# Cosine attention and an MLP mixer: residuals from DMA transposes, ScalarE norms, a permuted weight and two score tiles

## The chip, the cores and the metric

The kernel runs on one core of one Trainium2 chip. Time is device microseconds (us) of one execution. A fast run and a slow run are told apart: a run counts as slow when it took over 1.5% longer than the fastest run of the same kernel. Verdicts use the fast runs alone, with a 95% interval. The medians and ranges given in the tables are of all runs, slow ones included.

The engines are PE (TensorE, the matmuls), PEld (its weight loads, which overlap the matmuls), DVE (VectorE), ACT (ScalarE), POOL (GpSimd) and SP (SyncE, which here only issues DMAs). PEclk is the TensorE clock that was granted, as a share of full speed.

## The reference, cut to what matters

```python
# q, k, v: (8 batches, 12 heads, 448 rows, 64), float32
q_n = q / (norm(q) + 1e-6);  k_n = k / (norm(k) + 1e-6)
attn = softmax(q_n @ k_n.T / 0.1)
x = (attn @ v)                        # heads side by side: (8, 448, 768)

h = relu(x.T @ w_tok1) @ w_tok2       # 448 -> 256 -> 448, along the rows
u = x + h.T                           # first residual
h2 = relu(u @ w_ch1) @ w_ch2          # 768 -> 1536 -> 768, along the columns
out = u + h2                          # second residual
```

## The kernel before: the parts that the change touches

The kernel works through 48 pairs of heads, six to a batch. The schedule has one *slot* per pair. A slot scores one pair, applies the softmax weights of the pair before it, does the token mix of an earlier pair, and feeds matmuls of the channel mix of an earlier batch in between. I call the time from the first score matmul of one pair to that of the next the length of a slot.

Everything is fp16 on PE, with fp32 in PSUM. Both residuals are added on PE, by multiplying with an identity matrix into the PSUM tile that already holds the other term:

```python
ps2 = tile_pool(name="ps2", bufs=1, space=PSUM)      # one score tile of four banks

def rnorms(n, p0=0, p1=HP):                          # 1 / (norm + eps)
    nc.scalar.activation(out=rn, in_=ssq, func=AF.Ln, bias=tiny[:])
    nc.scalar.activation(out=rn, in_=rn, func=AF.Exp, scale=0.5)
    nc.vector.tensor_scalar_add(out=rn, in0=rn, scalar1=EPS_NORM)
    nc.vector.reciprocal(out=rn, in_=rn)

def score(i, cg):                                    # twice per pair
    psS = ps2.tile([128, 2, 2, 512], FP32, tag="s")
    ...                                              # four matmuls of 448 columns
    nc.scalar.activation(out=pt[:, cg], in_=psS[0:SC, :, :, 0:S], func=AF.Exp, scale=inv_tau)

def m_tok2(i):                                       # u, transposed, for one pair
    for tt in range(TT):
        nc.tensor.matmul(psU[:], r[:, tt, :], w2t[:, tt, 0:S], start=(tt == 0), stop=False)
    for c in range(NCH):                             # x residual: four identity matmuls,
        nc.tensor.matmul(psU[:].rearrange("d (p c) -> d c p", c=NCH)[:, c, :],   # every 4th column
                         x[:, c, :], id16[:, ...], start=False, stop=(c == NCH - 1))
    nc.vector.tensor_copy(out=ut[:, dt, 0:S], in_=psU[:])      # (odd batches: two parts)

def m_ch2(b, m, dh):                                 # one output unit, 56 in all
    for ct in range(CT):
        nc.tensor.matmul(psF[:], rows(gt, ct), wc2t[:, ct, ...], start=(ct == 0), stop=False)
    for i in range(3):                               # u residual: three identity matmuls
        nc.tensor.matmul(psF[:, 128 * i:128 * (i + 1)], rows(ut, 3 * dh + i), id16[:],
                         start=False, stop=(i == 2))
    if dh == 0: nc.vector.tensor_copy(out=o[:, 0:DH], in_=psF[:])
    else:       nc.scalar.copy(out=o[:, DH:D], in_=psF[:])
```

From pair 12 on the normalized q and k are already transposed by the DMA (`dma_start_transpose` issued by SP). Before that PE transposes them.

## Time and profile before

| | before |
|---|---|
| time, median of 3 runs (range) | 456.56 us (456.43 to 456.67) |
| PE busy, matmuls | 408.4 us of 455.0, 4104 |
| first matmul of the hidden layer (psG) | 67.0 us |
| first output unit starts (psF) | 107.2 us |
| last matmul starts | 450.1 us |

The windows view cuts the execution into stretches. Columns are the stretch, its length, then for PE, PEld, DVE, ACT and POOL the busy us (and the number of instructions), the granted PE clock, the mean busy share of the 16 DMA engines (the times of their packets are summed, so in a short stretch it can read above 1), and GB/s. The cuts are the second slot, a point just before the first hidden layer, the first output unit, and the start of the last pair.

```profile
core 0: us, PE busy (x) PEld busy (x) DVE busy (x) ACT busy (x) POOL busy (x), PEclk, DMA share, GB/s
0.00:21.30 21.30, 3.73 (x26) 1.90 (x27) 10.47 (x17) 8.36 (x13) 9.01 (x18) 1.00 0.98 230
21.30:66.60 45.30, 32.76 (x422) 23.08 (x423) 28.34 (x69) 26.17 (x28) 33.30 (x34) 0.96 0.98 211
66.60:107.20 40.60, 30.55 (x297) 17.50 (x297) 26.08 (x45) 20.52 (x30) 29.35 (x29) 0.87 0.61 125
107.20:396.70 289.50, 287.75 (x2954) 175.05 (x2952) 128.81 (x305) 166.52 (x182) 141.83 (x137) 1.00 0.53 124
```

The reader should see two regimes. From 107.2 us on PE is idle for 289.50 - 287.75 = 1.75 us: it alone sets the time there, and any matmul removed should come off the total. In the 107 us before that, PE is busy for only 67, and the time is set by chains of other engines.

One such chain is seen in the timeline of before (start, length, engine, line, operation, output and input, and in brackets the idle time before it and what ended it):

```profile
53.48 1.22 DVE L155 TENSOR_REDUCE ssq_130<-sq_609 112x16 f32<-112x1024 f32 x1 [0.57 <-POOL sq_609 L150]
54.73 0.31 ACT L162 ACTIVATE rn_131<-ssq_130,tiny 112x16 f32<-112x16 f32 x1 [2.21 <-DVE ssq_130 L155]
55.19 1.65 ACT L210 ACTIVATE pt_719<-psS_0_720 112x1792 f16<-112x1792 f32 x1
56.89 0.93 PE L208 MATMUL psS_1_769<-qk_660 64*128 64x448 f16 x4 [2.30 <-ACT pt_719 L210]
...
71.36 6.27 DVE L164 TENSOR_SCALAR rn_382<-rn_382 112x16 f32<-112x16 f32 x1 [0.62 <-ACT rn_382 L163]
71.57 1.05 POOL L176 TENSOR_TENSOR qn_924<-qh_378,rn_382 112x512 f16<-112x512 f32 x1
...
76.57 1.03 POOL L150 TENSOR_TENSOR sq_931<-kh_702 112x512 f32<-112x512 f32 x1
77.55 0.88 POOL L112 DMA_DIRECT2D wc2t<-in_moe_w_ch_dram  x1
77.66 0.25 DVE L165 RECIPROCAL rn_382<-rn_382 112x16 f32<-112x16 f32 x1
78.56 0.53 PE L188 MATMUL pst_990<-id_83,kn_817 112*128 112x112 f16 x4 [8.11 <-DVE x_950 L225]
```

The first four lines are the circle that paces the opening. ACT waits for DVE's sum of squares before it can take the norm, only then does the exponential of 1792 columns, and the second group of scores waits for that exponential. The other lines are an accident in it. A tiny DVE instruction, the addition of epsilon on 16 columns, takes 6.27 us while POOL runs six computing instructions without a gap, and it ends as the last of them ends. PE waits 8.11 us, until DVE has done what stood behind it. This fits what the Trainium skill, "SBUF — State Buffer", section "🔬 SBUF: two separate sides", describes: DVE and GpSimd share one pair of ports under an exclusive lock, and the loser fully blocks.

### The profile page before, as it was taken

The numbers are of one execution on the slowest core, as the hardware profiler recorded it, in microseconds if no ns is written. First come the engines' busy times: TensorE is split into PE (matmuls) and PEld (weight loads), VectorE is DVE, ScalarE is ACT, GpSimd is POOL, SyncE is SP. The second block draws the span as 40 slices with busy tenths as digits, with TensorE's granted clock in tenths as the row PEclk, the third lists the DMA queues.
The fourth block names the chain that finished last, engine by engine and source line by source line (L and its number), as shares of the span: only waits on it lengthen the run. The fifth ranks groups of instructions, "written<-read, shape, count | busy, mean of one in ns | idle before, by whom it ended". The sixth has DMA issues, their size and how long they took to land.

```text
span 455.0 us, 9700 instructions
## 1 busy us (share of the span) xinstructions
PE 408.4 (90%) x4104; PEld 250.4 (55%) x4104; DVE 202.8 (45%) x458; ACT 236.8 (52%) x277; POOL 213.5 (47%) x216
## 2 busy tenths in 40 slices
PE   1377572899999999999999999999999999999995
PEld 0146451466655666556655666556656665566563
DVE  3656758565444354444534445446343433232000
ACT  3466543475466545675466455665565447630410
POOL 2686779391919265563838091926474330000000
PEclk9999987899999999999999999999999999999998
DMA  8999877752775169662685279733852233001012
GB/s 212 250 254 239 145 182 109 141 134 71 176 177 154 27 179 159 168 161 68 167 177 143 61 134 218 193 86 98 195 83 77 58 110 56 1 1 71 35 51 89
DMA packets 76411, 58.11 MB, mean 128 GB/s; under 512 B 36976, under 2 KB 72784, under 8 KB 76368
## 3 DMA queue, kind: packets, MB, share of 16 engines
q1 hardware_dynamic: 72704, 52.32, 48.0%
q0 software_dynamic: 3664, 5.18, 6.9%
q8 instruction: 32, 0.52, 0.5%
q14 instruction: 11, 0.09, 0.1%
HBM read 43.38 MB, written 11.01 MB: 120 GB/s over the span
## 4 chain that ended last, share of the span: by engine, by line
PE 80%; DVE 7%; ACT 6%; POOL 4%; issue 2%; DMA 1%; SPq 0%; ACTq 0%; POOLq 0%
DVE rn_382 L164 1%; DVE ssq_130 L155 1%; DVE ssq_381 L155 1%; DMA kh_104<-in_k_dram 1%; ACT pt_308 L210 1%; DVE ssq_118 L155 1%; DVE ssq_704 L155 0%; PE psG_2_1016 L269 0%; PE psF_1_0_3760 L288 0%; PE psF_1_0_2231 L288 0%; PE psF_0_0_2105 L288 0%; PE psF_2_1_1719 L288 0%; PE psF_1_0_5275 L288 0%; PE psF_1_1_1595 L288 0%; PE psF_0_1_1466 L288 0%
## 5 line engine op out<-in xcount | busy, mean ns | idle before, releaser
L269 PEld LDWEIGHTS <-wc1t 128*128 128x128 f16 x576 | 53.8, 101 | 45.1 <-issue 7.2
L233 PEld LDWEIGHTS <-w1t 128*128 128x128 f16 x384 | 22.7, 98 | 0.0
L288 PEld LDWEIGHTS <-gt_0_449 128*128 128x128 f16 x168 | 15.7, 98 | 10.9 <-issue 1.9
L288 PEld LDWEIGHTS <-gt_3_4834 128*128 128x128 f16 x168 | 15.9, 98 | 9.3
L288 PEld LDWEIGHTS <-gt_1_1784 128*128 128x128 f16 x168 | 15.8, 98 | 9.4 <-issue 0.4
L288 PEld LDWEIGHTS <-gt_2_3305 128*128 128x128 f16 x168 | 15.7, 98 | 9.5 <-issue 0.4
L188 PE MATMUL pst_156<-id_83,kn_154 112*128 112x112 f16 x4 | 0.6, 294 | 9.0 <-DVE kn_154 L176 9.0
L294 DVE COPY ost_0_6217<-psF_0_0_6218 128x384 f32<-128x384 f32 x1 | 0.6, 559 | 17.3 <-PE psF_0_0_6218 L291 17.3
L188 PE MATMUL pst_990<-id_83,kn_817 112*128 112x112 f16 x4 | 0.5, 286 | 8.1 <-DVE x_950 L225 8.1
L164 DVE TENSOR_SCALAR rn_382<-rn_382 112x16 f32<-112x16 f32 x3 | 6.6, 2206 | 1.9 <-ACT rn_382 L163 1.9
L176 POOL TENSOR_TENSOR qn_5263<-qh_4628,rn_4632 112x512 f16<-112x512 f32 x1 | 1.0, 1043 | 13.5 <-DVE rn_4632 L165 13.5
L176 POOL TENSOR_TENSOR qn_3745<-qh_3099,rn_3103 112x512 f16<-112x512 f32 x1 | 1.0, 1042 | 13.5 <-DVE rn_3103 L165 13.5
L176 POOL TENSOR_TENSOR qn_2216<-qh_1570,rn_1574 112x512 f16<-112x512 f32 x1 | 1.0, 1043 | 12.4 <-DVE rn_1574 L165 12.4
L176 POOL TENSOR_TENSOR qn_4510<-qh_3880,rn_3884 112x512 f16<-112x512 f32 x1 | 1.0, 1042 | 12.4 <-DVE rec_0_4542 L224 12.4
L176 POOL TENSOR_TENSOR qn_2981<-qh_2351,rn_2355 112x512 f16<-112x512 f32 x1 | 1.0, 1042 | 11.3 <-DVE rec_0_3013 L224 11.3
L176 POOL TENSOR_TENSOR qn_2611<-qh_1952,rn_1956 112x512 f16<-112x512 f32 x1 | 1.0, 1042 | 11.1 <-DVE rn_1956 L165 11.1
L176 POOL TENSOR_TENSOR qn_1839<-qh_1193,rn_1197 112x512 f16<-112x512 f32 x1 | 1.0, 1042 | 10.5 <-DVE rn_1197 L165 10.5
L176 POOL TENSOR_TENSOR qn_1452<-qh_808,rn_812 112x512 f16<-112x512 f32 x1 | 1.0, 1042 | 10.1 <-PE psO_0_1485 L221 10.1
L162 ACT ACTIVATE rn_107<-ssq_106,tiny 112x16 f32<-112x16 f32 x3 | 0.9, 307 | 9.1 <-DVE ssq_106 L155 9.1
L176 POOL TENSOR_TENSOR qn_4132<-qh_3481,rn_3485 112x512 f16<-112x512 f32 x1 | 1.0, 1044 | 9.6 <-DVE rn_3485 L165 9.6
L188 PEld LDWEIGHTS <-kn_154 112*128 112x128 f16 x4 | 0.3, 130 | 9.0 <-DVE kn_154 L176 9.0
L176 POOL TENSOR_TENSOR qn_4889<-qh_4246,rn_4250 112x512 f16<-112x512 f32 x1 | 1.0, 1042 | 9.0 <-DVE rn_4250 L165 9.0
(1681 smaller groups left out, 1266.8 us busy)
## 6 DMA issues: line engine op xcount, KB each, us to landing
wc1t<-in_moe_w_ch_dram POOLq DMA_DIRECT2D x2, 1152.0 KB, 10.9
wc2t<-in_moe_w_ch_dram POOLq DMA_DIRECT2D x2, 1152.0 KB, 9.5
qh_103<-in_q_dram SPq DMA_DIRECT2D x3, 224.0 KB, 4.3
kh_104<-in_k_dram SPq DMA_DIRECT2D x3, 224.0 KB, 4.6
vs_105<-in_v_dram SPq DMA_DIRECT2D x1, 672.0 KB, 7.0
qh_115<-in_q_dram SPq DMA_DIRECT2D x3, 224.0 KB, 8.1
kh_116<-in_k_dram SPq DMA_DIRECT2D x3, 224.0 KB, 8.3
vs_117<-in_v_dram SPq DMA_DIRECT2D x1, 672.0 KB, 10.7
```

Source lines behind the costliest of these rows:

```text
L155: nc.vector.tensor_reduce(out=half[i // HP]["ssq"][:, :, lo:lo + 2 * NCH], in_=pipe[i]["sq"][:], axis=AXX.X, op=ALU.add)
L162: nc.scalar.activation(out=rn, in_=ssq, func=AF.Ln, bias=tiny[:])
L164: nc.vector.tensor_scalar_add(out=rn, in0=rn, scalar1=EPS_NORM)
L176: eng.tensor_tensor(out=dst[:].rearrange("p c g e -> p g c e"), in0=src, in1=_bcast_free(rn, E), op=ALU.mult)
L188: nc.tensor.transpose(pst[:, a, c, :], src[:, c], id16[:SC, :SC])
L210: nc.scalar.activation(out=st["pt"][:, cg], in_=psS[0:SC, :, :, 0:S], func=AF.Exp, scale=inv_tau)
L233: nc.tensor.matmul(psR[:, tt, :], w1t[:, m, tt * 128:(tt + 1) * 128], st["x"][:, m, :], start=(m == 0), stop=(m == NCH - 1))
L269: nc.tensor.matmul(psG[:], wc1t[:, dt, ct * 128:(ct + 1) * 128], ut[:, dt, span(b)], start=(dt == 0), stop=(dt == DT - 1))
L288: nc.tensor.matmul(psF[:], rows(gt, ct), wc2t[:, ct, dh * DH:(dh + 1) * DH], start=(ct == 0), stop=False)
L294: nc.vector.tensor_copy(out=o[:, 0:DH], in_=psF[:])
```

## The change

The intent is to take work off PE where PE sets the time, and to unblock the opening.

1. Output residual. u is transposed back into rows by the DMA, 48 transposes issued by SP, and DVE adds it when it copies the output out of PSUM. The 168 identity matmuls go.
2. x residual. For pairs 12 to 41 the DMA transposes x into columns (30 transposes) and DVE adds it when it writes u. Four identity matmuls per pair go. For these pairs the second token matmul is one slot later.
3. w_tok2's columns are permuted once on POOL, so that the residual matmuls that stay write contiguous PSUM columns. DVE puts u's columns back in order, by writing with a stride of four elements.
4. Norms. Ln and Exp on ACT replace DVE's addition and reciprocal.
5. Scores. Two PSUM tiles of two banks in turn, in place of one of four, with exponentials of 896 columns in place of 1792.
6. Schedule. Norms, squares and loads of the opening come earlier.

```diff
+    X_DMA = range(12, NP_ALL - NPAIR)
-    ps2 = ctx.enter_context(tc.tile_pool(name="ps2", bufs=1, space=bass.MemoryType.PSUM))
+    ps2 = ctx.enter_context(tc.tile_pool(name="ps2", bufs=2, space=bass.MemoryType.PSUM))
...
+    def place_w2():
+        for tt in range(TT):
+            nc.gpsimd.tensor_copy(out=w2t[:, tt], in_=w2n[:, tt].rearrange("t (p c) -> t c p", c=NCH))
...
-        nc.vector.tensor_scalar_add(out=rn, in0=rn, scalar1=EPS_NORM)
-        nc.vector.reciprocal(out=rn, in_=rn)
+        nc.scalar.activation(out=rn, in_=rn, func=AF.Ln, bias=eps[:])
+        nc.scalar.activation(out=rn, in_=rn, func=AF.Exp, scale=-1.0)
...
+    def x_tpose(i):
+        st["xT"] = att.tile([128, NCH, 128], FP16, name=f"xT_{i}", tag="xT")
+        nc.sync.dma_start_transpose(out=st["xT"][:], in_=st["x"][:].rearrange("p c d -> p (c d)"))
...  # m_tok2
-            nc.tensor.matmul(psU[:].rearrange("d (p c) -> d c p", c=NCH)[:, c, :], st["x"][:, c, :],
+        for c in range(0 if by_dma else NCH):
+            nc.tensor.matmul(psU[:, c, :], st["x"][:, c, :], id16[:, LEAD[c]:LEAD[c] + SC],
+                             start=False, stop=(c == NCH - 1))
...
+                nc.vector.tensor_tensor(
+                    out=ut[:, dt, lo:lo + n].rearrange("d (p c) -> d c p", c=NCH)[:, c0:c1],
+                    in0=psU[:, c0:c1, p0:p1], in1=st["xT"][:, c0:c1, r + p0:r + p1], op=ALU.add)
...
+        nc.sync.dma_start_transpose(out=urt[b][:, dt, 0:n], in_=ut[:, dt, lo:lo + 128 * n])
...  # m_ch2
-        for i in range(3):
-            nc.tensor.matmul(psF[:, 128 * i:128 * (i + 1)], rows(ut, 3 * dh + i), id16[:],
-                             start=False, stop=(i == 2))
+        nc.vector.tensor_tensor(out=o[:, dh * DH:(dh + 1) * DH].rearrange("p (i d) -> p i d", i=3),
+                                in0=psF[:].rearrange("p (i d) -> p i d", i=3),
+                                in1=urt[b][:, 3 * dh:3 * dh + 3, j, :], op=ALU.add)
...  # schedule
-    sq_at = at({p: p - 3 if p < 10 else max(p - 6, 2 + p // 2) for p in range(3, NP_ALL)})
+    sq_at = at({p: p - 4 if p < 12 else max(p - 6, (p + 2) // 2) for p in range(4, NP_ALL)})
+    rn_at = at({p: p - 3 if p < 12 else (p + 4) // 2 for p in range(3, 15)})
+    EARLY = 8                        # slots in which the scores are issued in smaller parts
```

## The prediction

> **What bounds it now.** Windows view: from 109.3 us (first output unit) to 395.1 us TensorE (PE) is busy 284.0 of 285.8 us, DVE 127.5, ACT 164.9, POOL 141.8, DMA 0.54. Starts of successive matmuls follow at their column rate, so PE alone bounds this stretch and the tail. Before 109.3 it does not: PE idles 17.6 us up to 21.3, 12.5 up to 66.6, 8.1 up to 85.7. There each pair slot lasts about 6.5 us, on a circle in the timeline: DVE sum -> ACT Ln/Exp, DVE add and reciprocal -> ACT exponential of 1792 (1.66 us) -> second score group, which needs the single four-bank PSUM tile (PE waits about 2.2 us). At 71.4 us one DVE TENSOR_SCALAR on the norms takes 6270 ns instead of 175 while POOL runs without a gap; PE waits 8.1 us, and the recorded clock is half speed from 73.7 to 84.0. This agrees with the Trainium skill, "SBUF — State Buffer", "Terms": DVE and GpSimd share an exclusively locked port pair and the loser blocks.
>
> **PE work removed** (start-to-start times in the trace):
> - output residual: 168 matmuls x 55.8 ns = 9.4 us, all after 109 us;
> - x residual: about 342 ns per pair (strided columns, three of four at 95 ns) x 30 pairs = 10.3 us;
> - remaining 18 pairs: contiguous PSUM columns through permuted w2, 342 -> about 220 ns = 2.2 us.
> Together 22 us, nearly all in PE-bound time, so nearly all should appear.
>
> **Opening.** Norms leave DVE (no blocked TENSOR_SCALAR), are issued earlier, and score tiles alternate. I expect 5.5 us slots, the second slot at 17 us instead of 21.3, the first hidden-layer matmul near 57 instead of 67, and no stall at 70-79. That is worth 10 + 8 us plus some half-clock time, less what DMA gives back: it is already 0.98 busy to 66.6 us, and 10 MB of weights must still come. I count 14 us net.
>
> **Added.** 78 DMA transposes (48 u, 30 x). A present one takes 448 packets of 29 ns = 0.81 us of all 16 engines and 1.26 us of SP issue. DMA share in the steady stretch goes to about 0.8; SP issue per slot rises from about 4 us to 6.6 of a 7.4 us slot, in order, with waits. That is the danger: a late x transpose holds a PSUM bank and the in-order DVE. I charge 2-3 us. DVE gains the second output half (28 x about 0.56 us) and two to four adds for u, loses the norms (20 us): flat. ACT loses 13.4 us of output copies and gains fixed cost of 96 more exponentials, about 18 us: flat, off the path.
>
> **Sum.** 456.6 - 22 - 14 + 2.5 = 423 us. Range 409 to 438. Faster by over 2%: 0.96; same 0.03; slower 0.01.
>
> **What would show it.** PE start-to-start unchanged per kind and 288 matmuls fewer (4104 -> 3816); PE still over 97% busy from the first output unit to the end; steady slot 7.4 us instead of 7.94; no DVE instruction over 2 us; first hidden-layer matmul at 53 to 62 us; SP issuing 80-90% of the time, DMA 0.75-0.85; u copies waiting on x transposes in few slots.
>
> **What would make it wrong.** SP or DMA falls behind: waits of PE for q/k transposes, of DVE for xT, slots near 8 us, a result near 437. Or the opening is held by loads and POOL (squares of three pairs fall in one slot around pair 7), so only 5 us is gained. Or it compresses fully, giving 410. DVE adds with one PSUM and one SBUF operand might also meet the port lock.

## The result, and the profile after

The changed kernel took 430.34 us (428.43 to 431.24, 4 runs), and the kernel before, on the same chip, 456.5 us (456.25 to 456.67, 4 runs). The ratio is 0.9422, with a 95% interval from 0.939 to 0.9454. A ratio here is the mean time of one kernel's fast runs over that of the other's of the same rounds, so it is not quite the ratio of the medians. All runs of all kernels in this document agreed with the reference.

So the kernel is faster, inside the range, and 7 us above the predicted 423. The windows of after, cut at the same events:

```profile
0.00:19.10 19.10, 3.83 (x24) 1.96 (x25) 8.44 (x10) 10.32 (x25) 11.77 (x20) 1.00 0.96 218
19.10:59.40 40.30, 32.08 (x420) 20.76 (x419) 34.90 (x56) 30.20 (x57) 34.92 (x36) 0.92 1.04 204
59.40:93.60 34.20, 30.18 (x300) 17.19 (x298) 18.72 (x36) 22.87 (x44) 25.86 (x25) 0.90 0.95 191
93.60:371.30 277.70, 268.95 (x2704) 153.67 (x2702) 149.86 (x346) 163.66 (x253) 142.42 (x137) 1.00 0.83 164
```

Three things differ. The first output unit comes at 93.6 us, 13.6 us earlier than before. The DMA share in the steady stretch rose from 0.53 to 0.83. And PE, which was idle for 1.75 us of that stretch, is now idle for 277.70 - 268.95 = 8.75 us.

The busy time of overlapping matmuls does not add up to PE's real load, so I also took the starts of all matmuls from the trace. From the first output unit to the last matmul, every gap between two successive starts was compared with the usual gap for those two kinds of matmul. What exceeds it is a *stall*. The rest is PE's own work.

| us | before | after | difference |
|---|---|---|---|
| first output unit starts | 107.2 | 93.6 | -13.6 |
| PE work from there to the last matmul | 340.8 | 318.5 | -22.3 |
| stalls in the same stretch | 2.1 | 10.7 | +8.6 |
| last matmul starts | 450.1 | 422.8 | -27.3 |

The last row is the sum of the three above. This is the whole result in one table: both gains came as large as predicted (14 and 22), and stalls grew by 8.6 us where 2 to 3 had been charged.

Where do the stalls come from? In the list of gaps about 6.0 us follow ACT being late: 4.4 us in four places (near 144, 189, 212 and 306 us) where norms stand in front of the exponentials, and 1.6 us in four smaller gaps without norms. About 4.7 us follow a DMA transpose being late, in four gaps. In the kernel before, all 2.1 us were of ACT's kind. One place of the first kind, in the timeline of after:

```profile
140.89 1.21 DVE L164 TENSOR_REDUCE ssq<-sq 112x16 f32<-112x1024 f32 x1
142.13 0.34 ACT L171 ACTIVATE rn<-ssq,tiny 112x48 f32<-112x48 f32 x1 [3.64 <-DVE ssq L164]
143.29 3.32 ACT L221 ACTIVATE pt<-psS 112x896 f16<-112x896 f32 x4
144.24 0.36 PE L219 MATMUL psS<-qk 64*128 64x448 f16 x2 [0.36 <-ACT pt L221]
145.04 0.36 PE L219 MATMUL psS<-qk 64*128 64x448 f16 x2 [0.44 <-ACT pt L221]
```

ACT is in order. The four norm instructions stand ahead of the exponentials and wait 3.64 us for DVE's sum. The exponentials start late, and the scores wait for the PSUM tiles that they free.

And one of the second kind. The `SPq` lines are SP's queue of DMA issues:

```profile
310.71 2.53 SPq L207 DMA_TRANSPOSE qk<-kn  x1
313.30 1.25 SPq L207 DMA_TRANSPOSE qk<-qn  x1
314.64 1.48 SPq L242 DMA_TRANSPOSE xT<-x  x1
316.17 1.19 SPq L135 DMA_DIRECT2D qh<-in_q_dram  x1
317.41 0.45 SPq L135 DMA_DIRECT2D kh<-in_k_dram  x1
317.96 0.40 SPq L331 DMA_DIRECT2D out_dram<-ost  x1
318.46 1.30 SPq L298 DMA_TRANSPOSE ur<-ut  x1
...
319.39 0.56 PE L219 MATMUL psS<-qk 64*128 64x448 f16 x4 [1.21 <-DMA qk<-qn]
319.89 1.15 DVE L279 TENSOR_TENSOR ut<-psU,xT 128x336 f16<-128x336 f32 x2 [6.04 <-DMA xT<-x]
```

SP issues one DMA after the other without a gap. Here a transpose holds it for 1.25 to 2.5 us, a plain DMA for 0.4 to 1.2 (over the whole steady stretch a transpose takes 1.25 us at the median, and 4.1 us at most). In the stretch from the first output unit to the last pair SP's issues add up to 0.865 of the time, against 0.46 before. The x transpose is issued late, lands late, and DVE, which is in order, stands still for 6.04 us. PE waits for q's transpose (1.21 us), then for the buffers that DVE would free.

The waits view of after (who waited for what: us in total, times, longest) shows both:

```profile
DVE ut L279 <- DMA xT<-x: 21.1, 7, 6.0
PE psS L219 <- ACT pt L221: 10.9, 16, 4.8
```

The chain of waits that ended last, as shares of the span, first before, then after. Before:

```profile
PE 80%; DVE 7%; ACT 6%; POOL 4%; issue 2%; DMA 1%; SPq 0%; ACTq 0%; POOLq 0%
```

After:

```profile
PE 65%; DMA 11%; DVE 7%; ACT 5%; POOL 5%; issue 3%; SPq 3%; POOLq 0%; DVEq 0%
```

DMA and SP's queue went from 1% of the chain to 14%. In the chain of the kernel before they hardly appeared. Not all of this is transposes: by line, the page gives 5% to loads of q (most of it in the opening), 2% to loads of v and 3% to x transposes.

Two groups of instructions of after, by shape (count, then busy us and mean ns of one, then idle time before them), show a cost that I had not counted:

```profile
L284 DVE CAST ut<-psU 128x448 f16<-128x448 f32 x6 | 6.9, 1161 | 2.6 <-PE psU L274 2.6
L279 DVE TENSOR_TENSOR ut<-psU,xT 128x336 f16<-128x336 f32 x18 | 16.5, 914 | 28.3 <-PE psU L271 15.3 <-DMA xT<-x 8.6 <-PE psG L304 4.4
```

The same copy of 448 columns took 624 ns in the kernel before, where it wrote u contiguously. The write with a stride of four elements makes it 1161 ns. DVE's busy time rose from 202.8 to 226.6 us, where I had it flat. DVE is busy for 0.54 of the steady stretch, so this alone does not set the time.

### The profile page after: what moved, and what is told of

It reads as the page before. It is cut to its first block, busy times and chain, and to the rows that moved or that the text cites. A ratio compares the mean times of both kernels' runs of the same rounds, so it can differ in the third digit from the quotient of the medians.

```text
span 428.0 us, 9442 instructions
## 1 busy us (share of the span) xinstructions
PE 386.8 (90%) x3816; PEld 224.0 (52%) x3816; DVE 226.6 (53%) x478; ACT 239.4 (56%) x397; POOL 215.0 (50%) x217
## 2 busy tenths in 40 slices
DMA packets 115770, 67.53 MB, mean 158 GB/s; under 512 B 76336, under 2 KB 112144, under 8 KB 115728
## 4 chain that ended last, share of the span: by engine, by line
PE 65%; DMA 11%; DVE 7%; ACT 5%; POOL 5%; issue 3%; SPq 3%; POOLq 0%; DVEq 0%
PE psF L323 22%; PE psG L304 20%; PE psO L232 8%; PE psS L219 7%; DMA qh<-in_q_dram 5%; PE psU L271 4%; ACT pt L221 4%; PE psR L249 3%; DMA xT<-x 3%; POOL sq L158 3%; DVE ssq L164 2%; DMA vs<-in_v_dram 2%; DVE kn L185 2%; DVE ut L279 1%; SPq L135 1%
## 5 line engine op out<-in xcount | busy, mean ns | idle before, releaser
L221 ACT ACTIVATE pt<-psS 112x896 f16<-112x896 f32 x192 | 163.9, 914 | 60.9 <-PE psS L219 60.8
L304 PE MATMUL psG<-ut,wc1t 128*128 128x448 f16 x576 | 123.7, 355 | 2.0 <-DVE rec L235 2.0
L323 PE MATMUL psF<-wc2t,gt 128*128 128x384 f16 x672 | 117.2, 326 | 0.0
L185 POOL TENSOR_TENSOR qn<-qh,rn 112x512 f16<-112x512 f32 x46 | 48.0, 1043 | 105.6 <-ACT rn L174 95.9
L306 ACT ACTIVATE gt<-psG 128x448 f16<-128x448 f32 x96 | 51.8, 545 | 71.1 <-PE psG L304 70.6
L323 PEld LDWEIGHTS <-gt 128*128 128x128 f16 x672 | 63.2, 98 | 41.1 <-issue 2.7
L219 PE MATMUL psS<-qk 64*128 64x448 f16 x384 | 59.2, 369 | 16.3 <-ACT pt L221 10.9
L232 PEld LDWEIGHTS <-pt 112*128 112x128 f16 x1536 | 61.4, 99 | 19.2 <-issue 7.3
L232 PE MATMUL psO<-vt,pt 112*128 112x65 f16 x1536 | 66.6, 196 | 0.0
L164 DVE TENSOR_REDUCE ssq<-sq 112x16 f32<-112x1024 f32 x48 | 58.0, 1210 | 11.7 <-POOL sq L158 6.7
L158 POOL TENSOR_TENSOR sq<-kh 112x512 f32<-112x512 f32 x46 | 49.2, 1069 | 1.5 <-DMA kh<-in_k_dram 1.5
L219 PEld LDWEIGHTS <-qk 64*128 64x128 f16 x384 | 13.6, 95 | 47.2 <-issue 34.8
## 6 DMA issues: line engine op xcount, KB each, us to landing
wc2t<-in_moe_w_ch_dram POOLq DMA_DIRECT2D x2, 1152.0 KB, 12.6
```

The costliest lines, as they stand in the source:

```text
L158: nc.gpsimd.tensor_mul(out=sq[:, a], in0=src, in1=src)
L164: nc.vector.tensor_reduce(out=half[i // HP]["ssq"][:, :, lo:lo + 2 * NCH], in_=pipe[i]["sq"][:], axis=AXX.X, op=ALU.add)
L185: eng.tensor_tensor(out=dst[:].rearrange("p c g e -> p g c e"), in0=src, in1=_bcast_free(rn, E), op=ALU.mult)
L219: nc.tensor.matmul(psS[:, hh, 0:S], qk[hb:hb + 64, c * SC:c * SC + 128], qk[hb:hb + 64, S:2 * S], start=True, stop=True)
L221: nc.scalar.activation(out=st["pt"][:, c], in_=psS[0:SC, :, 0:S], func=AF.Exp, scale=inv_tau)
L232: nc.tensor.matmul(psO[:, m, 0:E + 1], st["pt"][:, c, hh, lo:lo + 128], vt[:, g, c, 0:E + 1], start=(c == 0), stop=(c == NCH - 1))
```

## The experiments

The theory: PE's work fell as predicted, and the missing microseconds are stalls, of two kinds. (A) The norms stand in front of the exponentials on ACT. (B) SP's in-order queue is too full, so transposes are late. Rivals: for (B), that the 16 DMA engines are too full (0.83), not SP; for the opening, that the score tiles, not the norms and the order of work on POOL, made it faster; and that the loss is DVE's strided writes.

Each edit is against the changed kernel unless it says otherwise. Ranges and numbers of runs are in brackets. The kernel before ran in the same jobs, with medians of 456.50, 455.56, 456.98 and 456.15 us, so ratios compare across jobs. After itself has 0.9422 [0.939, 0.9454].

### x_none and u_none: undo one residual

```diff
-    X_DMA = range(12, NP_ALL - NPAIR)
+    X_DMA = ()                                    # x_none
```

> x residual of batches 2 to 6 put back on TensorE (four identity matmuls a pair, but now with contiguous PSUM columns), everything else as changed. Theory A (w2's permutation had already made these matmuls cheap, 49 ns each as in the 18 pairs that kept them, and the x transposes cost TensorE stalls through late xT): +5.9 us of matmuls, about 4 to 5 us of stalls gone, 429 to 433 us. Rival B (the prediction's costing, 342 ns a pair gained by the x transposes): about 440 us. Rival C (all new stalls come from the norms, none from the x transposes): about 436 us.

Without x transposes the second token matmul of these pairs also returns to the slot that it had before the change.

u_none puts the three identity matmuls and the two copies of m_ch2 back and takes away the u transposes:

```diff
-        nc.sync.dma_start_transpose(out=urt[b][:, dt, 0:n], in_=ut[:, dt, lo:lo + 128 * n])
...
+        for i in range(3):
+            nc.tensor.matmul(psF[:, 128 * i:128 * (i + 1)], rows(ut, 3 * dh + i), id16[:],
+                             start=False, stop=(i == 2))
```

> Output residual put back on TensorE (168 identity matmuls, evacuation by DVE copy and ScalarE copy), x transposes kept. Theory A: 168 x 55.8 ns = 9.4 us more TensorE work; 48 transposes fewer give DMA and the SP queue relief, so 1 to 4 us of stalls go: 436 to 439 us. Rival: no stall depends on these transposes, 440 us or more.

| us | after | x_none | u_none |
|---|---|---|---|
| time, median (range; runs) | 430.34 (428.43 to 431.24; 4) | 431.39 (428.32 to 432.13; 6) | 433.97 (432.84 to 434.58; 6) |
| ratio to before [95%] | 0.9422 | 0.9451 [0.9413, 0.9488] | 0.9516 [0.9481, 0.9551] |
| PE work from the first output unit | 318.5 | 324.4 | 327.9 |
| stalls | 10.7 | 6.0 | 5.1 |
| SP's issue share | 0.865 | 0.666 | 0.632 |

The gross gain of u's transposes is 9.4 us of PE work, exactly 168 matmuls of 55.8 ns. That is the time per matmul of 128 columns that the Trainium skill gives, "TensorE: Matmul & The Clock Gate", section "Wait — 56ns, not 53.3ns?", and this trace agrees. The gross gain of x's transposes is 5.9 us, 30 pairs of four matmuls of 49 ns. Undoing either takes about half of the stalls away, so the net worth is much smaller: 9.4 - 5.6 = 3.8 us for u, and 5.9 - 4.7 = 1.2 us for x, which the times don't tell from nothing (the intervals overlap). u_none came out 2 us below the range expected for it: more stalls went than the 1 to 4 us of theory A. The two sets of transposes pay for each other's delays.

The rest of PE's gain, 22.3 - 9.4 - 5.9 = 7.0 us, is the permuted w2. That is a remainder, since no run undoes the permutation alone, but it agrees with the starts in the traces: with contiguous PSUM columns the four residual matmuls of a pair take about 196 ns from start to start, where they took about 342 before, and 48 pairs of 146 ns are 7.0 us.

### norm_late: take the norms from in front of the exponentials

From slot 12 on, the norms of three pairs are issued on ACT after the next slot's first exponentials, when DVE's sum is ready.

```diff
-            if i:
+            if 0 < i < 12:
                 gpsimd_part(i)
...
+            if i >= 12:                            # after score(i, 0, 2)
+                for p in sq_at.get(i - 1, ()):
+                    if p >= 15 and p % HP == HP - 1:
+                        rnorms(p // HP)
+                gpsimd_part(i)
```

> From slot 12 on the four norm activations of a half are issued after the first two exponentials of the next slot instead of before them; the GpSimd work of a slot follows them. Theory A (ScalarE stands in order before the sums of VectorE, so exponentials start about 3 us late in one slot of three and TensorE waits for score banks, about 1 us each): 4 to 6 us faster, 424 to 427 us, and the gaps of TensorE before score matmuls of the third and fourth tile vanish in the steady stretch. Rival: those gaps come from late q/k transposes or DMA load; then unchanged, 430 us.

Measured 430.01 us (428.7 to 434.5, 6 runs), ratio 0.944 [0.9396, 0.9485]: no gain. The profiled run was its slowest, at 434.5 us, with the clock at 0.64 of full speed from 322 to 330 us. In it the gaps that came from the norms are gone, and PE's wait for the exponentials fell from 10.9 to 6.8 us in the waits view. But the stalls are 12.8 us: the gaps of late transposes near 201, 223 and 318 us grew. The wait behind took over what the one in front had hidden. That by itself shows neither theory right, and the stalls of this slowest run may be more than usual. It asks for both to be removed at once (best_c, below).

### loads_act: take the loads off SP's queue

From pair 18 on, the plain loads of q, k and v are issued by ACT. The packets are the same, so the DMA engines do the same work (115,771 packets in all against 115,770).

```diff
-            nc.sync.dma_start(out=half[n][nm][:, j:j + 2]...
+            (nc.scalar if i >= 18 else nc.sync).dma_start(out=half[n][nm][:, j:j + 2]...
```

> q, k (from pair 18) and v (from half 6) loads issued from the ScalarE queue instead of SP; same bytes on the same 16 DMA engines. Theory A (issue time of the SP queue, 87% of the steady stretch, makes the x transposes late): SP falls to about 75%, waits of DVE for xT fall from 21 us to under 8, 2 to 4 us faster, 426 to 428 us. Rival (the 16 DMA engines at 0.84 make them late): xT waits and time unchanged, 430 us, or slower because ScalarE pays the issue time.

Measured 436.7 us (434.39 to 437.73, 6 runs), ratio 0.9567 [0.9529, 0.9605]: 6 us slower. Still, it tells something. SP's issue share fell from 0.865 to 0.657, and DVE no longer waits for any x transpose (21.1 us in after; one wait of 1.4 us is left, put down to ACT). So with the DMA engines doing the same work, the late x transposes are gone. That speaks for SP's queue as cause (B). The traces also say on which part of the way the time was lost. In after, 8.4 us pass at the median from DVE's last write of x to the issue of its transpose; here it is 3.5 us. From issue to landing (minimum, median and maximum in us, by the view of line L242) the transposes did not become faster but slower. In after:

```profile
DMA to landing us min/median/max: 2.4/3.0/6.7
```

In loads_act:

```profile
DMA to landing us min/median/max: 2.4/4.3/9.6
```

So in after they were issued late, and not slow once issued. The price is that ACT pays for the issues. Scores' stalls grew from 7.3 to 12.6 us. I moved the loads and not the transposes on purpose: the Trainium skill, "DMA: Bandwidth & Descriptors", section "Silent corruption: two transposing streams in flight at once", warns against DMA transposes from two engines at a time. No run here tests that.

### norm_dve and one_tile: which part of the opening matters

```diff
-        nc.scalar.activation(out=rn, in_=rn, func=AF.Ln, bias=eps[:])      # norm_dve
-        nc.scalar.activation(out=rn, in_=rn, func=AF.Exp, scale=-1.0)
+        nc.vector.tensor_scalar_add(out=rn, in0=rn, scalar1=EPS_NORM)
+        nc.vector.reciprocal(out=rn, in_=rn)
```

> Norms back on VectorE (add of eps and reciprocal instead of the second Ln and Exp), the changed kernel's new issue order and two-tile scores kept. Theory A (the move to ScalarE is what took the blocked TENSOR_SCALAR out of the opening): one or more of these adds again last over 2 us while GpSimd runs without a gap, first output unit 3 to 8 us later than 93.6, total 433 to 438 us. Rival B (the new issue order did it; the add would no longer meet a busy GpSimd): no add over 1 us, and the steady stretch gains 1 to 2 us because ScalarE has two activations fewer before the exponentials: 427 to 430 us.

```diff
-    ps2 = ... bufs=2 ...                                                   # one_tile
+    ps2 = ... bufs=1 ...
+        psS = ps2.tile([128, 2, 2, 512], FP32, name=f"psS_{i}_{c0}", tag="s")
...
-    EARLY = 8
+    EARLY = 0
```

> Scores back to one PSUM tile of four banks with one exponential of 1792 columns and two score groups a slot, all else as changed. Theory A (the alternating tiles break the wait of the second score group on ScalarE): opening slots 5 to 8 take about 6 us instead of 4.5, first output unit at 98 to 102 us instead of 93.6, total 435 to 439 us. Rival B (the opening is set by DVE, GpSimd and loads, not by the score tiles): first output unit within 2 us of 93.6, total 429 to 433 us.

one_tile has the score tile and the exponentials of before and everything else of after. It took 428.92 us (425.61 to 431.24, 4 runs), ratio 0.9405 [0.9332, 0.9477]: the same as after. Its first output unit came at 91.1 us, against 93.6. So the two-tile scores (with their issue in smaller parts, EARLY), which the prediction named as one cause of the faster opening, are not one.

norm_dve's fast runs took 437.08, 432.8 and 434.01 us, ratio 0.954 [0.9476, 0.9605]: 5 us slower than after. Its profiled run was a slow one (442.36 us), so I don't compare its times, but the mechanism shows in its timeline:

```profile
79.75 8.17 DVE L173 TENSOR_SCALAR rn<-rn 112x16 f32<-112x16 f32 x1 [0.73 <-ACT rn L172]
86.43 1.45 POOL L144 CAST vt<-vs 112x1536 f16<-112x1536 f32 x1
87.95 0.25 DVE L174 RECIPROCAL rn<-rn 112x16 f32<-112x16 f32 x1
```

The blocked addition is back, this time for 8.17 us (an earlier one, at 35.07 us, takes 3.86), and in that slow run the first output unit starts at 106.2 us, while the stretch after it is as long as in after (328.9 against 329.2 us). So moving the norms to ACT is worth about 5 us by the fast runs, and what the one profile shows of it lies in the opening.

### spread and k_pool: what still holds the opening

After's slots 5 to 7 are 4.2 to 4.5 us long. Slot 8 then takes 14.1 us: POOL squares three pairs in slot 7 that the loads have only just brought. spread puts the squares and norms of pairs 13 and 14 one slot later. k_pool takes the scaling of k off DVE, where two instructions were blocked for 3.67 and 3.06 us.

```diff
-    sq_at = at({p: p - 4 if p < 12 else max(p - 6, (p + 2) // 2) for p in range(4, NP_ALL)})
-    rn_at = at({p: p - 3 if p < 12 else (p + 4) // 2 for p in range(3, 15)})
+    sq_at = at({p: p - 4 if p < 12 else {12: 7, 13: 8, 14: 9}.get(p, p - 6) for p in range(4, NP_ALL)})
+    rn_at = at({p: p - 3 if p < 12 else p - 4 for p in range(3, 15)})      # spread
```

> Squares, sums and norms of pairs 13 and 14 one slot later, so that no slot holds the squares of three pairs (slot 7 had 11, 12 and 13). Theory A (VectorE stands in order before the third sum, whose squares wait for GpSimd, and TensorE waits for it about 4 us in slot 8): slot 8 takes about 10 us instead of 14.1, total 426 to 428 us. Rival B (in that window the DMA engines are full, share above 1.0, and the data come when they come): slot 8 shorter but slots 9 and 10 longer, total 429 to 431 us.

```diff
-            scaled(p, dve="k" if p < 7 else "")
+            scaled(p, dve="")                                              # k_pool
```

> Scaling of k in pairs 2 to 6 on GpSimd instead of VectorE. Theory A (these two-input VectorE multiplies meet GpSimd's port lock, 3.67 and 3.06 us instead of 0.68, and TensorE waits 3 to 4 us twice): no VectorE instruction over 2.5 us, slots 2 and 4 of 6.6 and 9.9 us shrink to about 5.5, total 426 to 428 us. Rival B (GpSimd is itself the limit of these slots and takes 1.04 us more in each): slots 1 to 5 together as long or longer, total 430 to 433 us.

spread took 424.4 us (421.68 to 426.72, 4 runs), ratio 0.9314 [0.9251, 0.9376]. Its first output unit starts at 88.4 us, 5.2 us earlier than after's. Slot 8 in the windows view, first of after, then of spread. After:

```profile
59.40:73.50 14.10, 10.08 (x83) 5.55 (x81) 7.30 (x12) 8.55 (x20) 12.03 (x12) 0.76 1.14 243
```

spread:

```profile
60.80:68.30 7.50, 7.15 (x82) 4.36 (x80) 6.04 (x11) 7.18 (x16) 7.50 (x8) 1.00 1.29 237
```

About the same number of matmuls takes 7.50 us in place of 14.10, and PE ran at full clock in place of 0.76. The Trainium skill, "TensorE: Matmul & The Clock Gate", section "What's actually happening", says that an idle window halves the clock. This trace agrees: after an idle time of 3.68 us in slot 8 the recorded clock is half, and six matmuls of the hidden layer take 2.45 us in place of 1.30. The idle time is paid a second time in clock.

k_pool took 434.08 us (429.82 to 434.3, 4 runs), ratio 0.9506 [0.9447, 0.9565]: no gain, and probably about 4 us slower (its interval just overlaps after's), although no DVE instruction lasts over 1.53 us any more. Its profiled run is the fastest of the four, no slower than after, so the profile can't show where the 4 us went. In it slots 1 to 7 are 2.6 us shorter together, but slot 8 grew to 18.4 us. There POOL waits for loads:

```profile
61.02 1.04 POOL L158 TENSOR_TENSOR sq<-qh 112x512 f32<-112x512 f32 x1 [3.08 <-DMA qh<-in_q_dram]
63.31 1.04 POOL L158 TENSOR_TENSOR sq<-kh 112x512 f32<-112x512 f32 x1 [1.25 <-DMA kh<-in_k_dram]
65.94 1.04 POOL L158 TENSOR_TENSOR sq<-qh 112x512 f32<-112x512 f32 x1 [1.59 <-DMA qh<-in_q_dram]
67.68 1.04 POOL L158 TENSOR_TENSOR sq<-kh 112x512 f32<-112x512 f32 x1 [0.71 <-DMA kh<-in_k_dram]
```

It reaches the squares of pairs 12 and 13 sooner and then stands idle for 6.6 us until their q and k land. Unblocking the early slots is not a gain when the loads of a later slot come no sooner.

### best_a to best_d: both causes at once

best_a is spread, k_pool and norm_late together. I included k_pool in the hope that it would help once spread had relieved POOL.

> spread + k_pool + norm_late together. Theory A (each removes one wait, and the one behind it was what gave the gain back): spread 5 us, k_pool about 3 us of opening no longer lost in slot 8, norm_late 2 to 5 us: first output unit at 84 to 87 us, 417 to 422 us. Rival: they do not add up because loads hold the opening and SP the rest, 423 to 425 us.

best_b is best_a, with the loads of q, k and v from pair 18 on issued by POOL instead of SP:

```diff
+            (nc.gpsimd if i >= 18 else nc.sync).dma_start(out=half[n][nm][:, j:j + 2]...   # q, k
+        (nc.gpsimd if n >= 6 else nc.sync).dma_start(out=half[n]["vs"][:]...              # v
```

> As best_a, with the q, k loads from pair 18 and v loads from half 6 issued from the GpSimd queue. Theory A (SP issue, 87% and with no gap in the bad places, makes transposes late): SP near 75%, TensorE stalls after the first output unit under 4 us, 3 to 5 us faster than best_a. Rival B (the DMA engines themselves are late): equal to best_a within 1.5 us. Rival C (GpSimd pays too much for issuing): slower than best_a.

best_c is best_a with `X_DMA = ()`, that is without x transposes.

> As best_a, with the x residual on TensorE (no x transposes). Theory A: 5.9 us more matmuls, but with the norms out of the way almost no stall is left (under 2 us after the first output unit, against 6.0 in x_none), so equal to best_a within 2 us. Rival: stalls stay near 6 us, 4 us or more slower than best_a.

best_d is best_b without k_pool.

> best_b without k_pool: spread + norm_late + loads on the GpSimd queue, k of pairs 2 to 6 scaled on VectorE again. Theory A (k_pool only makes slots 1 to 7 shorter and slot 8 longer, because loads of pairs 12 and 13 hold slot 8; in spread alone the first output unit came at 88.4 us against 90.5 in best_a): first output unit 1 to 3 us earlier than best_b's 90.9, total 417 to 420 us against 420.7. Rival (the 3 us port-lock waits cost what they show): 423 us or more.

| | time, us (range; runs) | ratio [95%] | first output unit | PE work after it | stalls |
|---|---|---|---|---|---|
| after | 430.34 (428.43 to 431.24; 4) | 0.9422 [0.939, 0.9454] | 93.6 | 318.5 | 10.7 |
| best_a | 429.03 (425.88 to 430.51; 6) | 0.9371 [0.9332, 0.9409] | 90.5 | 318.8 | 9.8 |
| best_b | 420.74 (418.57 to 421.5; 5) | 0.919 [0.9159, 0.9222] | 90.9 | 318.3 | 2.5 |
| best_c | 424.02 (418.87 to 427.44; 6) | 0.9236 [0.9189, 0.9282] | 92.7 | 324.3 | 0.9 |
| best_d | 417.93 (415.37 to 426.16; 6) | 0.9136 [0.9103, 0.9169] | slow run | slow run | slow run |

best_a's gain over after is unclear: the intervals overlap, and its stalls hardly moved. It is outside both expected ranges, and no better than spread alone. best_b and best_c settle the cause, from two sides (their profiled runs took 418.57 and 425.03 us, best_a's 426.32):

- best_c takes the x transposes away and gains 5 us over best_a, where no gain was expected, although PE has 5.5 us more to do. Stalls fall from 9.8 to 0.9 us.
- best_b keeps all transposes and takes only the loads off SP. It gains 8 us. Stalls fall to 2.5 us, and SP's issue share from 0.855 to 0.726.

In best_b the steady stretch looks like this, and so does its chain of waits:

```profile
90.90:360.20 269.30, 267.53 (x2702) 152.72 (x2698) 150.90 (x346) 163.81 (x253) 189.70 (x206) 1.00 0.92 168
```

```profile
PE 81%; POOL 6%; DVE 4%; DMA 3%; ACT 2%; issue 2%; SPq 0%; POOLq 0%; ACTq 0%
```

PE is idle for 1.77 us of the stretch, as in the kernel before (1.75), and PE work is that of after. DMA fell from 11% of the chain to 3%, nearly all loads of q. And the DMA share *rose*, from 0.83 to 0.92. If full DMA engines had made the transposes late, this kernel would be worse. It is the best so far. The rival for (B) falls. So does the third rival: DVE still does all the strided writes, 150.90 us busy against 149.86.

The 2 by 2 of stalls shows why norm_late alone gained nothing:

| stalls, us | norms in front | norms late |
|---|---|---|
| with x transposes, loads on SP | 10.7 (after) | 12.8 (norm_late), 9.8 (best_a) |
| without x transposes | 6.0 (x_none) | 0.9 (best_c) |

With the norms cured, late transposes make stalls of the same size. With the transposes gone, ACT's gaps leave 6.0 us. Only both together bring them near zero. best_a and best_c also contain spread and k_pool, whose edits act before the first output unit, where these stalls are not counted.

best_d, without k_pool, is the fastest: 417.93 us, 3% below after and 8.6% below before. Two of its six runs were slow by the rule (422.97 and 426.16 us), and one of them was the profiled one, so its profile is not used. Its interval just overlaps best_b's, so that dropping k_pool was worth 2 us is likely, not certain. k_pool's own run points the same way, with intervals that just overlap as well. The median of best_d's four fast runs is 416.09 us.

Loads that leave SP also leave its hardware queue, so it could have been the order of the data in that queue and not SP's issuing. The traces speak against that: in best_b the time from x to the issue of its transpose fell from 8.4 to 3.5 us at the median, while issue to landing rose from 3.0 to 4.6:

```profile
DMA to landing us min/median/max: 2.4/4.6/10.0
```

What stays open is why some issues last up to 4.1 us. POOL's loads also use fewer packets (101,211 in all against 115,770), which could have helped best_b; in loads_act, where the packets were the same, the waits for x transposes were gone too. Moving the issue costs POOL: a load of q takes it 694 ns and one of k 674 ns, and its busy time in the execution went from 215.0 to 265.6 us. The Trainium skill, "DMA: Bandwidth & Descriptors", section "Issuing engines are not separate DMA queues", says that issuing from several engines only saves the time on the sequencer, usually small beside the DMA itself. The traces agree with the first half as far as they go: the transposes were issued sooner and landed no faster. Here that time was not small: one issue takes 1.25 us against 3.0 us to landing, and from best_a to best_b the change of queue was worth 8 us of 429, fewer packets included.

## Why the prediction was right or wrong

The time (423 us, 409 to 438) held: 430.34, faster by over 2%. Point by point:

- "Together 22 us" of PE work: right, 22.3, and as a division by pairs the parts fit too (9.4, 30 pairs of 342 ns, and 2.6 us where 2.2 stood for the other 18 pairs). They don't tell what each edit is worth, though. x's transposes removed only 5.9 us and the permutation of w2 7.0 us, because with the permutation the alternative to a transpose is a contiguous set of matmuls, which costs 196 ns a pair and not 342.
- "nearly all should appear": wrong. From the first output unit to the last matmul 342.9 became 329.2 us, so 13.7 of 22.3 us appeared.
- "I count 14 us net" for the opening: right, 13.6, but partly by luck. The first hidden-layer matmul came 6.6 us earlier and the stretch from there to the first output unit became 7.0 us shorter, where 10 and 8 less a guess for DMA had been counted, and the second slot began at 19.1 us and not at 17. Of its causes, "no blocked TENSOR_SCALAR" was one (norm_dve, about 5 us), and "score tiles alternate" was not (one_tile, same time). The named risk, "squares of three pairs fall in one slot around pair 7", was real: spread gained about 5 us. How the remaining gain is divided among the earlier norms and loads no run here shows.
- "I charge 2-3 us" for SP, DMA and DVE: this is the step that failed. Stalls grew by 8.6 us: those that follow late transposes measured 4.7 us, against none before, and ACT's the rest. The danger was named ("SP issue per slot ... in order, with waits"), and SP's share (0.865) and the DMA share (0.83) came out in the predicted bands. What was too low is what such a full queue costs. A transpose of x was issued 8.4 us after x was ready, and 3.5 us after with the loads off SP. The wait for the x transposes was 21.1 us in only 7 places, and there it held up DVE, and PE behind it.
- ACT's part in the stalls was not in the sum at all: 6.0 us, against 2.1 before. ACT was called "flat, off the path". Its busy time was flat (236.8 to 239.4 us), but the norms in front of the exponentials became a wait of PE, 4.4 us in four places.
- "PE still over 97% busy from the first output unit": wrong. It is 268.95 of 277.70 us, 96.8%, up to the last pair, and 320.76 of 334.40, 95.9%, to the end, a sign of the same stalls. "steady slot 7.4 us instead of 7.94": from slot 12 to slot 47 it is 7.86 us where before had 8.19, a gain of 0.33 us per slot where 0.54 was forecast.
- "288 matmuls fewer (4104 -> 3816)" and "first hidden-layer matmul at 53 to 62 us": right, 3816 and 60.4 us.
- "no DVE instruction over 2 us": wrong. Scaling k, with two inputs in SBUF, took 3.67 us once and 3.06 us once beside POOL.
- DVE "flat": wrong, 202.8 to 226.6 us. The writes of u, strided and with the added x, take 69.0 us in sum where they took 33.5. It had no visible price.

## What to carry to other kernels

Work that is moved from a saturated engine to the DMA must be costed on the queue that issues it, in order, not only on the DMA engines: with 0.865 of SP's time spent on issues, and with the norms ahead of the exponentials, stalls took back 8.6 of the 22.3 us that PE had been spared. Moving plain loads to POOL's queue, and the norms behind the exponentials, gave most of it back; on ACT's queue the loads cost 6 us. When two waits lie behind each other, removing one can show nothing; test them alone and together before either is cleared. And price each part of a change against the kernel that the other parts leave, not against the old one: the permuted weight leaves the x transposes 5.9 us to gain of the 10.3 that they would have had alone.

## What the Trainium skill lacked or had wrong

- "DMA: Bandwidth & Descriptors", "Issuing engines are not separate DMA queues", calls the sequencer's issue time usually small. Here an SP issue of a DMA transpose took 1.18 to 4.13 us of SP, 1.25 at the median, with 134 of them in the steady stretch, and moving loads from SP to POOL was worth 8 us (best_a to best_b). I found no time for the issue of a transpose on the page that could have been used here.
- "SBUF — State Buffer", "🔬 SBUF: two separate sides", says that the lock is held for the whole instruction. In these traces the loser stayed blocked over several: a DVE instruction waited 6.27 us across six POOL instructions of about 1.04 us each (before, 71.36 us), and went on when POOL came to a DMA issue.
- No page that I used has the price in time of a matmul's strided PSUM output: an identity matmul of 112 columns took 95 ns from start to start (three of four) with every fourth fp32 column, and 49 ns with contiguous ones.
- No page that I used has the price of a strided fp16 write by DVE: a copy of 128x448 from PSUM took 1161 ns with a stride of four elements, and 624 ns without.
- "TensorEngine Tiling (Array Packing)", "Performance Considerations", gives no time for going between matmuls of 64 rows and of 128. Here each change cost about 95 ns from start to start (281 to 285 ns after a matmul of 448 columns that otherwise takes 189).
